# Retention block with two MLPs: sums on VectorE, operand tiles at multiples of 1,024 bytes, scratch in the output staging

## The chip, the core and the metric

One core of a Trainium2 chip runs the whole program: one launch, all inputs in HBM, the result in HBM. The metric is device time in microseconds, as a median of several executions. One further execution is recorded by the hardware profiler; every row below is of that one.

## The reference

```python
def _attn_ref(q, k, v):                       # 4 x 8 heads x 576 x 64
    scores = scale * np.matmul(q, k.transpose(0, 1, 3, 2))
    gamma = 1.0 - 2.0 ** (-5.0 - np.arange(H))
    Dmat = np.where(rel >= 0, gamma[:, None, None] ** rel[None], 0.0)
    return np.matmul(scores * Dmat[None], v)

def _moe_ref(x, w_in, w_out):                 # 2304 x 512, 512 x 2048, 2048 x 512
    h = np.maximum(x @ w_in, 0.0)
    return h * h @ w_out

def _moe2_ref(x, w_gate, w_val, w_out):       # 2304 x 512, 512 x 1536 (twice), 1536 x 512
    g = x @ w_gate
    silu = g * (1.0 / (1.0 + np.exp(-g)))
    return silu * (x @ w_val) @ w_out

def reference(q, k, v, ...):
    x = _attn_ref(q, k, v).transpose(0, 2, 1, 3).reshape(2304, 512)
    return _moe2_ref(_moe_ref(x, ...), ...)
```

## The kernel before

**Three passes for one product.** Operands of the MLPs are kept as pairs, a high part and the rest. `three` (L176 to L178) multiplies a pair by a pair with three matmuls: high by high, high by low, low by high. The moving operand comes from one SBUF tile and the stationary one from another.

**The weights** arrive as 64-bit numbers. `round32` turns a raw tile of 1,024 columns into 32-bit floats (two ScalarE steps, L214 and L219; four VectorE steps, L222, L225, L231, L234), and `split` (L252 on ScalarE, L256 on VectorE) makes the pair. For the first MLP the pairs stay in SBUF (`convert1`, 16 tiles `w`). For the second they go to DRAM (`keep`), twelve gate/value tiles (`convert_gv`) and six output tiles (`convert_out`), while the first MLP runs. `convert_gv` also makes four sums of quarter tiles, at L295, on GpSimd (POOL).

**First part.** Eighteen cells of retention (128 rows each) are woven between the blocks of the first MLP. A block is 512 rows, one of the five 256. For each of 16 slices `f`, `mlp1_h` does 12 matmuls from the tile `x` into the single PSUM bank `hps`; `mlp1_act` does the rest (`relu` on ScalarE into a scratch tile, `square`, `hi`, `lo` on VectorE) and writes the pair `h`; `mlp1_y` does 12 matmuls from `h` into four banks `acc`. In both the weights `w` are the stationary operand. Block results go by way of `yd` in DRAM.

**Second part.** Three blocks of 768 rows times twelve slices make 36 steps. A step's gate and value products are done as seven half-size products (`PRODUCTS`, `mlp2_gv`, matmuls 128x384 from the tiles `xc`), whose sums VectorE takes from PSUM in turn into the banks' successors; then come six pieces of the output product (`mlp2_o`, 128x512, L806 to L808), two steps late. Step 1 has no such pieces, and step 0 has the last pieces of the first MLP. `fetch_x` makes the seven operand tiles `xc` of a block from `yd`: four differences at L621 on GpSimd, seven splits. `xc` has NX = 9 places; part `n` takes the place of part `n - NX`, after that one's last product.

**Order.** `Plan` writes the whole instruction order. Each operation has an engine, an assumed time, dependencies and a rank; a list scheduler picks the operation that can start earliest, the lowest rank first among those that are ready. Every engine then runs its list in order. A 512-column matmul is assumed at 0.2264 us.

**Where tiles lie.** Pools stack from both ends of a partition. The left stack begins at byte 1,152: 1,024 of DMA scratch, and four constants of 32 each. Then come `x` (2 tiles of 16,384), `h` (2 of 4,096), the scratch `tp`, and the staging. The right stack begins at byte 229,344 and grows down, first `pad` (32 bytes), then the weight tiles, 8,192 bytes each. So in the first part `x` and `h` start 128 bytes past a multiple of 1,024, and the weight columns that one matmul loads (512 bytes) start 960 or 448 past one. In the second part `xc`, the weight ring and `at` all lie in the right stack, at 960 or 448 past a multiple.

Of the kernel before, what the change touches and what calls it, by code (L numbers as in the profile page):

```python
# [10 lines left out]
F32 = mybir.dt.float32  # L11
# [17 lines left out]
T2, N2 = 6, 3  # L29
# [11 lines left out]
         ("V", 1), ("raw", 1), ("A", 2), ("q", 2), ("V", 2), ("A", 3), ("q", 3), ("V", 3)]  # L41
PRODUCTS = [("A11", "B11"), ("A12", "B21"), ("S2", "T2"), ("S1", "T1"), ("S3", "T3"), ("S4", "B22"), ("A22", "T4")]
PLAIN, SUMS = ["A11", "A12", "A22"], ["S1", "S2", "S3", "S4"]
NX, NRING = 9, 7
INSERTS = {2: (4, 10), 4: (2, 6, 10, 13)}


# [90 lines left out]
def kernel(ctx: ExitStack, tc: tile.TileContext, units, qtab, tab, w1, w2, out):  # L138
# [11 lines left out]
    do = Plan()  # L150

    pad = ctx.enter_context(tc.tile_pool(name="pad", bufs=1, side="right"))
    pad.tile([128, 8], F32, name="pad")
    wp = ctx.enter_context(tc.tile_pool(name="wp", bufs=NW1 - NA, side="right"))
    wstack = ExitStack()
    wa = wstack.enter_context(tc.tile_pool(name="wa", bufs=NA, side="right"))
    xp = ctx.enter_context(tc.tile_pool(name="xp", bufs=2))
    hp = ctx.enter_context(tc.tile_pool(name="hp", bufs=2))
    tp = ctx.enter_context(tc.tile_pool(name="tp", bufs=1))
    io = ctx.enter_context(tc.tile_pool(name="io", bufs=2))  # L160
    sp = ctx.enter_context(tc.tile_pool(name="sp", bufs=1))
    cv = ctx.enter_context(tc.tile_pool(name="cv", bufs=1))
# [85 lines left out]
    def split(get, n, out, place, rank, deps, cols=None):  # L248

        def hi():  # L250
            out["t"] = place()
            nc.scalar.copy(out=out["t"][:, 0], in_=get())  # L252

        def lo():
            t = out["t"]
            nc.vector.tensor_tensor(out=t[:, 1], in0=get(), in1=t[:, 0].bitcast(F32), op=ALU.subtract)  # L256

        h = do("ACT", 0.17 + 0.43 * n / 512, hi, deps, rank)
        return do("DVE", 0.16 + 0.53 * n / 512, lo, [h], rank)
# [24 lines left out]
    def convert_gv(box, f, rank):  # L284


        st, p4 = round32(box, rank)
        a21, a11, a12, a22 = (slice(256 * i, 256 * i + 256) for i in range(4))

        def add(i, a, b, op, new=False):  # L290
            def go():
                if new:
                    st["s"] = cv.tile([128, 4, 256], F32, tag="r", name="s")
                x, y = (st["s"][:, k] if isinstance(k, int) else st["fm"][:, k] for k in (a, b))
                nc.gpsimd.tensor_tensor(out=st["s"][:, i], in0=x, in1=y, op=op)  # L295
            return go

        s = do("POOL", 0.7, add(0, a21, a22, ALU.add, True), [p4], rank)
        s = do("POOL", 0.7, add(1, 0, a11, ALU.subtract), [s], rank)
        s = do("POOL", 0.7, add(2, a11, a21, ALU.subtract), [s], rank)  # L300
        s = do("POOL", 0.7, add(3, a12, 1, ALU.subtract), [s], rank)
        l = keep("P", f, st, 768, lambda: st["fm"][:, 256:], rank, [p4])
        f_users.append(do("NONE", 0.0, lambda: None, [s, l]))
        r_users.append(keep("S", f, st, 1024, lambda: st["s"].rearrange("p a b -> p (a b)"), rank, [s, l]))
# [189 lines left out]
    def mlp1_act(j, f):  # L494
        n = BLOCKS[j][1] * C
        i = at1[j, f]
        k = n / 512
        st = {}
        on_act = j in (0, NB - 1)

        def relu():
            st["r"] = tp.tile([128, n], F32, tag="t", name="r")
            nc.scalar.activation(out=st["r"], in_=banks[0][:, :n], func=ACTF.Relu)  # L503

        def square():
            if on_act:
                nc.scalar.activation(out=st["r"], in_=st["r"], func=ACTF.Square)
            else:
                nc.vector.tensor_tensor(out=st["r"], in0=st["r"], in1=st["r"], op=ALU.mult)  # L509

        def hi():
            Hs[j, f] = hp.tile([128, 2, n], F32R, tag="h", name="h")
            nc.scalar.copy(out=Hs[j, f][:, 0], in_=st["r"])  # L513

        def lo():
            nc.vector.tensor_tensor(out=Hs[j, f][:, 1], in0=st["r"], in1=Hs[j, f][:, 0].bitcast(F32), op=ALU.subtract)  # L516

        a = do("ACT", 0.17 + 0.43 * k, relu, [h_op[j, f], hlo_op.get(order1[i - 1]) if i else None], -3)
        relu_op[j, f] = a
        if on_act:  # L520
            b = do("ACT", 0.19 + 0.43 * k, square, [a], -2)
        else:
            b = do("DVE", 0.16 + 0.53 * k, square, [a], -2)
        c = do("ACT", 0.19 + 0.43 * k, hi, [b, y_op.get(order1[i - 2]) if i > 1 else None], -2)
        hlo_op[j, f] = do("DVE", 0.16 + 0.53 * k, lo, [c], -2)
# [80 lines left out]
    def fetch_x(b, rank):  # L606

        st = {}

        def load():  # L610
            st["t"] = xp.tile([128, KC + 1, T2 * C], F32, tag="x", name="ys")
            nc.sync.dma_start(out=st["t"][:, :KC], in_=y_dram[b])

        def at(name):
            if name == "T2":
                return st["t"][:, KC].rearrange("p (k n) -> p k n", k=2)
            k, h = {"B11": (0, 0), "B12": (0, 1), "B21": (2, 0), "B22": (2, 1), "T1": (0, 0), "T3": (0, 1), "T4": (2, 0)}[name]
            return st["t"][:, k:k + 2, h * HALF:h * HALF + HALF]

        def sub(o, a, c):  # L620
            return lambda: nc.gpsimd.tensor_tensor(out=at(o), in0=at(a), in1=at(c), op=ALU.subtract)  # L621

        free = [h_op[NB - 2 + b, NF1 - 1]] if b < 2 else [("ysdone", b - 2)]
        ready = {}
        ld = do("SP", 0.4, load, [*y_saved[b], *free, late["open"]], rank, kb=1536)

        def part(i, name, deps):
            n = 7 * b + i
            old = M_op[((n - NX) // 7) * NF2 + NF2 - 1, (n - NX) % 7] if n >= NX else late["open2"]
            out = {}  # L630

            def place():
                XC[b, name] = late["xc"].tile([128, 2, 2, HALF], F32R, tag="xc", name="xc")
                return XC[b, name]

            x_op[b, i] = l = split(lambda: at(name), 2 * HALF, out, place, rank, [*deps, old, *x_chain[-1:]])
            x_chain.append(l)
            return l

        b11 = part(0, "B11", [ld])  # L640
        b21 = part(1, "B21", [ld])
        t1 = do("POOL", 1.95, sub("T1", "B12", "B11"), [b11], rank)
        t2 = do("POOL", 1.95, sub("T2", "B22", "T1"), [t1], rank)
        t3 = do("POOL", 1.95, sub("T3", "B22", "B12"), [t1], rank)
        t4 = do("POOL", 1.95, sub("T4", "B21", "T2"), [t2, b21], rank)
        part(2, "T2", [t2])
        part(3, "T1", [t1])
        part(4, "T3", [t3])
        part(5, "B22", [t3])
        do.named["ysdone", b] = part(6, "T4", [t4])  # L650
# [35 lines left out]
    def mlp2_gv(s, pieces):  # L686
# [15 lines left out]

        def copy(name, bank, pool):
            def go():
                st[name] = late[pool].tile([128, HALF], F32, tag="t" if pool == "tp" else name, name=name)
                nc.scalar.copy(out=st[name], in_=late[bank][:, :HALF])
            return go

# [48 lines left out]

        other(0)
        product(0, "MA", [("c21", s - 1), late["open2"]])
        m1 = do("ACT", act, copy("m1", "MA", "tp"), [M_op[s, 0], ("u2", s - 1) if s else hlo_op[order1[-1]]], -3)  # L760
        product(1, "MB", [("c12", s - 1)])
        c11_ = name("c11", do("DVE", dve, c11, [M_op[s, 1], m1, g_op[s - 2] if s > 1 else y_op[order1[s - 2]]], -3))
        sg = do("ACT", act, sig(0, lo_half), [c11_, ("si1", s - 1)], -2)
# [170 lines left out]
    for j in range(NB):  # L934
# [3 lines left out]
        if not more:  # L938
            def swap():
                astack.close()  # L940
                late["tl"] = ctx.enter_context(tc.tile_pool(name="tl", bufs=1, reuse_waits="tile"))
                pgv = ctx.enter_context(tc.tile_pool(name="pgv", bufs=1, space=PSUM, reuse_waits="tile"))
                late["MA"], late["MB"], more = (pgv.tile([128, 512], F32, name=f"gv{i}") for i in range(3))
                late["more"] = [banks[0], more]
                late["tp"] = tp

            def swap2():
                wstack.close()
                for key, bufs in (("xc", NX), ("rg", 1), ("at", 2), ("tm", 1)):
                    late[key] = ctx.enter_context(tc.tile_pool(name=key, bufs=bufs, side="right", reuse_waits="tile"))  # L950

            late["open"] = do("NONE", 0.0, swap, [*(x for xs_ in x_done.values() for x in xs_), *(st_op[c] for c in range(NC))])
            late["open2"] = do("NONE", 0.0, swap2, [late["open"], y_op[NB - 1, NA - 1]])
# [25 lines left out]
    for s in range(steps2):  # L979
        b, f = divmod(s, NF2)  # L980
        mlp2_gv(s, last_y if s == 0 else () if s == 1 else mlp2_o(s - 2))
        if s == 0:
            fetch_x(0, 60)
        if f == 1 and b + 1 < N2:
            fetch_x(b + 1, 4)
    for s in (steps2 - 2, steps2 - 1):
        for piece in mlp2_o(s):
            piece()
# [69 lines left out]
```

## Time and profile before

| what | us |
|---|---|
| median of 3 runs (lowest to highest) | 931.86 (931.78 to 934.02) |
| profiled execution | 934.56 |
| its span, first to last instruction | 932.8 |
| PE busy in it | 909.2 |
| DVE, ACT, POOL busy | 593.8, 362.3, 120.5 |

The profiled execution lies 2.7 us above the median. PE is TensorE's matmuls, PEld its weight loads, DVE is VectorE, ACT ScalarE, POOL GpSimd. Matmuls overlap in the record: one lasts 0.28 to 0.40 us, while the next begins 0.11 to 0.23 us after it. So what a matmul costs in a stream is read from the starts of successive ones in the timeline, not from its duration. A row of the stretches view gives, for each engine, the busy time in that stretch and the count of instructions, and then TensorE's granted clock, where 1.00 is its upper level (2.4 GHz).

### The profile page before, as it was taken

The page shows a single profiled execution, that of the slowest core. Times are in us where ns is not written, and L with a number is a line of the kernel's source. Part 1 is how long each engine was busy: PE and PEld are TensorE (multiplying, and loading weights), DVE is VectorE, ACT ScalarE, POOL GpSimd, SP SyncE. Part 2 cuts the span into 40 slices and gives each one's busy share as a digit, 9 for nine tenths or more (in the row PEclk, how much of TensorE's full clock was granted, in tenths as well). Part 3 has the DMA queues.
Part 4 walks back from the last instruction along what each step waited for, and adds up shares of the span by engine and source line. Part 5 has one row for each costly group of instructions (what it writes and reads, how often), then busy time and mean ns, then how long its engine had stood idle before and what let it go on. Part 6 is the DMA issues. An engine that isn't in the chain of part 4 may idle for free.

```text
span 932.8 us, 12545 instructions
## 1 busy us (share of the span) xinstructions
PE 909.2 (97%) x4953; PEld 793.7 (85%) x4953; DVE 593.8 (64%) x872; ACT 362.3 (39%) x546; POOL 120.5 (13%) x97
## 2 busy tenths in 40 slices
PE   8899999999999999999999999998999999999997
PEld 7688879988878778878887899998999999999996
DVE  5999836457773777736455655569655557655554
ACT  3678743234541445446553222223222223322221
POOL 3210102112431312301133000003000000000000
PEclk9999999999999999999999999999999999999999
DMA  8665605337673567645436754555555455745521
GB/s 350 226 208 185 227 36 185 123 109 265 236 260 102 177 232 296 226 173 220 181 131 250 297 207 188 219 203 203 199 222 209 187 225 207 277 187 224 208 115 68
DMA packets 36634, 187.49 MB, mean 201 GB/s; under 512 B 4192, under 2 KB 5984, under 8 KB 22624
## 3 DMA queue, kind: packets, MB, share of 16 engines
q1 hardware_dynamic: 36576, 186.70, 53.7%
q8 instruction: 39, 0.64, 0.3%
q14 instruction: 19, 0.16, 0.1%
HBM read 148.93 MB, written 37.75 MB: 200 GB/s over the span
## 4 chain that ended last, share of the span: by engine, by line
PE 88%; DVE 6%; DMA 2%; ACT 2%; issue 2%; SPq 0%; ACTq 0%; DVEq 0%
PE gv L178 9%; PE gv L177 9%; PE gv L176 9%; PE acc L177 7%; PE hps L176 7%; PE acc L176 7%; PE acc L178 7%; PE hps L178 6%; PE hps L177 6%; PE acc L807 4%; PE acc L808 4%; PE acc L806 3%; DMA raw<-w 2%; PE xs L427 2%; PE sc L390 2%
## 5 line engine op out<-in xcount | busy, mean ns | idle before, releaser
L176 PE MATMUL gv<-xc,w 128*128 128x384 f32 x504 | 170.2, 338 | 5.8 <-DVE u L731 3.4
L177 PE MATMUL gv<-xc,w 128*128 128x384 f32 x504 | 171.3, 340 | 0.0
L178 PE MATMUL gv<-xc,w 128*128 128x384 f32 x504 | 171.0, 339 | 0.0
L176 PE MATMUL acc<-h,w 128*128 128x512 f32 (+1 forms) x320 | 119.5, 373 | 2.9 <-ACT yt L573 2.2
L177 PE MATMUL acc<-h,w 128*128 128x512 f32 (+1 forms) x320 | 119.5, 373 | 2.6 <-DVE h L516 2.5
L176 PE MATMUL hps<-x,w 128*128 128x512 f32 (+1 forms) x320 | 120.8, 378 | 1.0 <-ACT r L503 1.0
L177 PE MATMUL hps<-x,w 128*128 128x512 f32 (+1 forms) x320 | 119.1, 372 | 0.9 <-DVE x L452 0.9
L178 PE MATMUL hps<-x,w 128*128 128x512 f32 (+1 forms) x320 | 119.0, 372 | 0.0
L178 PE MATMUL acc<-h,w 128*128 128x512 f32 (+1 forms) x320 | 118.9, 372 | 0.0
L176 PEld LDWEIGHTS gv<-xc,w 128*128 128x128 f32 x504 | 95.5, 189 | 15.7 <-DVE u L731 4.6
L177 PEld LDWEIGHTS gv<-xc,w 128*128 128x128 f32 x504 | 95.3, 189 | 8.2
L736 ACT ACTIVATE sg<-g 128x384 f32<-128x384 f32 x72 | 37.8, 525 | 162.9 <-DVE g L728 131.5
L178 PEld LDWEIGHTS gv<-xc,w 128*128 128x128 f32 x504 | 95.4, 189 | 0.0
L503 ACT ACTIVATE r<-hps 128x512 f32<-128x512 f32 (+1 forms) x80 | 44.4, 555 | 127.1 <-PE hps L178 116.9
L516 DVE TENSOR_TENSOR h<-r,h 128x512 fp32r<-128x512 f32 (+1 forms) x80 | 55.6, 695 | 59.5 <-ACT h L513 59.0
L176 PEld LDWEIGHTS acc<-h,w 128*128 128x128 f32 x320 | 60.1, 188 | 15.9 <-ACT yt L573 2.9
L177 PEld LDWEIGHTS acc<-h,w 128*128 128x128 f32 x320 | 60.1, 188 | 15.3 <-DVE h L516 4.1
L176 PEld LDWEIGHTS hps<-x,w 128*128 128x128 f32 x320 | 60.1, 188 | 14.8 <-ACT r L503 1.9
L177 PEld LDWEIGHTS hps<-x,w 128*128 128x128 f32 x320 | 60.2, 188 | 12.1 <-DVE x L452 1.2
L178 PEld LDWEIGHTS hps<-x,w 128*128 128x128 f32 x320 | 60.1, 188 | 11.5
L178 PEld LDWEIGHTS acc<-h,w 128*128 128x128 f32 x320 | 60.1, 188 | 11.4
L509 DVE TENSOR_TENSOR r<-r 128x512 f32<-128x512 f32 (+1 forms) x48 | 33.2, 692 | 48.2 <-ACT r L503 48.2
(106 smaller groups left out, 1486.6 us busy)
## 6 DMA issues: line engine op xcount, KB each, us to landing
w<-wdS SPq DMA_DIRECT2D x36, 1024.0 KB, 5.7
raw<-w SPq DMA_DIRECT2D x34, 1024.0 KB, 4.8
w<-wdP SPq DMA_DIRECT2D x36, 768.0 KB, 5.8
w<-wdO SPq DMA_DIRECT2D x18, 1024.0 KB, 4.8
wdS<-cw SPq DMA_DIRECT2D x12, 1024.0 KB, 4.2
wdP<-cw SPq DMA_DIRECT2D x12, 768.0 KB, 3.4
qk<-units SPq DMA_DIRECT2D x14, 512.0 KB, 4.4
kv<-units SPq DMA_DIRECT2D x14, 512.0 KB, 3.9
```

The lines of the kernel that those rows point to most:

```text
L176: nc.tensor.matmul(ps, lhsT=wh, rhs=xh, start=first, stop=False)
L177: nc.tensor.matmul(ps, lhsT=wh, rhs=xl, start=False, stop=False)
L178: nc.tensor.matmul(ps, lhsT=wl, rhs=xh, start=False, stop=last)
L390: nc.tensor.matmul(s[h][:, p], lhsT=A[c][r, p, 1], rhs=A[c][r, p, 0], start=True, stop=True)
L427: nc.tensor.matmul(bank("xo")[r, p], lhsT=V[c][:, p, 1, r], rhs=P[c][:, h, p], start=c in FIRST and p == 0, stop=p == NP - 1)
L503: nc.scalar.activation(out=st["r"], in_=banks[0][:, :n], func=ACTF.Relu)
L509: nc.vector.tensor_tensor(out=st["r"], in0=st["r"], in1=st["r"], op=ALU.mult)
L516: nc.vector.tensor_tensor(out=Hs[j, f][:, 1], in0=st["r"], in1=Hs[j, f][:, 0].bitcast(F32), op=ALU.subtract)
L736: nc.scalar.activation(out=t, in_=st["g"][:, r], func=ACTF.Sigmoid)
L806: nc.tensor.matmul(ps, lhsT=at[:, 0, sl], rhs=wh, start=f == 0, stop=False)
L807: nc.tensor.matmul(ps, lhsT=at[:, 0, sl], rhs=wl, start=False, stop=False)
L808: nc.tensor.matmul(ps, lhsT=at[:, 1, sl], rhs=wh, start=False, stop=f == NF2 - 1)
```

## The change

- The sums of `convert_gv` (L295) and the differences of `fetch_x` (L621) are issued on VectorE and no longer on GpSimd.
- `pad` grows to 992 bytes and a `pad2` of 896 bytes opens the left stack. `x` then starts at byte 2,048, the weight stack ends at 228,352; all of `x`, `h`, `w`, `xc`, `at` start at multiples of 1,024, and single operands within them at 0 or 512 past one.
- The pool `tp` goes. The first MLP's scratch comes from `io`, the output staging (two tiles), and the second's `m1` from `tl`.
- `NX` is 11: nine places of `xc` as before and two (`xl`) in the left stack, where the retention's tiles were.
- Blocks 1 and 2 of the second MLP are fetched at rank 60 and not 4; their last three parts stay at 4.

```diff
-NX, NRING = 9, 7
+NX, NXL, NRING = 11, 2, 7
...
-    pad.tile([128, 8], F32, name="pad")
+    pad.tile([128, 248], F32, name="pad")
     wp = ctx.enter_context(tc.tile_pool(name="wp", bufs=NW1 - NA, side="right"))
     wstack = ExitStack()
     wa = wstack.enter_context(tc.tile_pool(name="wa", bufs=NA, side="right"))
+    ctx.enter_context(tc.tile_pool(name="pad2", bufs=1)).tile([128, 224], F32, name="pad2")
     xp = ctx.enter_context(tc.tile_pool(name="xp", bufs=2))
     hp = ctx.enter_context(tc.tile_pool(name="hp", bufs=2))
-    tp = ctx.enter_context(tc.tile_pool(name="tp", bufs=1))
...
-                nc.gpsimd.tensor_tensor(out=st["s"][:, i], in0=x, in1=y, op=op)
+                nc.vector.tensor_tensor(out=st["s"][:, i], in0=x, in1=y, op=op)
...
-        s = do("POOL", 0.7, add(0, a21, a22, ALU.add, True), [p4], rank)
+        s = do("DVE", 0.43, add(0, a21, a22, ALU.add, True), [p4], rank)
...
-            st["r"] = tp.tile([128, n], F32, tag="t", name="r")
+            st["r"] = io.tile([128, n], F32, tag="io", name="r")
...
-            return lambda: nc.gpsimd.tensor_tensor(out=at(o), in0=at(a), in1=at(c), op=ALU.subtract)
+            return lambda: nc.vector.tensor_tensor(out=at(o), in0=at(a), in1=at(c), op=ALU.subtract)
...
-                XC[b, name] = late["xc"].tile([128, 2, 2, HALF], F32R, tag="xc", name="xc")
+                XC[b, name] = late["xl" if n % NX < NXL else "xc"].tile([128, 2, 2, HALF], F32R, tag="xc", name="xc")
...
-            x_op[b, i] = l = split(lambda: at(name), 2 * HALF, out, place, rank, [*deps, old, *x_chain[-1:]])
+            x_op[b, i] = l = split(lambda: at(name), 2 * HALF, out, place, min(rank, 4) if b and i >= NX - 7 else rank,
+                                    [*deps, old, *x_chain[-1:]])
...
-        t1 = do("POOL", 1.95, sub("T1", "B12", "B11"), [b11], rank)
+        t1 = do("DVE", 0.96, sub("T1", "B12", "B11"), [b11], rank)
...
-        m1 = do("ACT", act, copy("m1", "MA", "tp"), [M_op[s, 0], ("u2", s - 1) if s else hlo_op[order1[-1]]], -3)
+        m1 = do("ACT", act, copy("m1", "MA", "tl"), [M_op[s, 0], ("u2", s - 1) if s else hlo_op[order1[-1]]], -3)
...
-                late["tl"] = ctx.enter_context(tc.tile_pool(name="tl", bufs=1, reuse_waits="tile"))
+                for key, bufs in (("tl", 1), ("xl", NXL)):
+                    late[key] = ctx.enter_context(tc.tile_pool(name=key, bufs=bufs, reuse_waits="tile"))
...
-                for key, bufs in (("xc", NX), ("rg", 1), ("at", 2), ("tm", 1)):
+                for key, bufs in (("xc", NX - NXL), ("rg", 1), ("at", 2), ("tm", 1)):
...
-            fetch_x(b + 1, 4)
+            fetch_x(b + 1, 60)
```

## Rows read from the trace of the kernel before

**Rows 1.** The page's first part: busy time, share of the span and instructions.

```profile
PE 909.2 (97%) x4953; PEld 793.7 (85%) x4953; DVE 593.8 (64%) x872; ACT 362.3 (39%) x546; POOL 120.5 (13%) x97
```

**Rows 2.** The chain that ended last, by engine.

```profile
PE 88%; DVE 6%; DMA 2%; ACT 2%; issue 2%; SPq 0%; ACTq 0%; DVEq 0%
```

**Rows 3.** Waits of PE alone: who for whom, us in total, times, longest.

```profile
PE gv L176 <- DVE u L731: 3.4, 2, 2.3
PE acc L177 <- DVE h L516: 2.5, 3, 1.4
```

**Rows 4.** Stretches: blocks 0, 2 and 3; steps 0-1, 2-11 and 12-13.

```profile
31.85:130.85 99.00, 97.36 (x488) 78.19 (x486) 83.60 (x103) 74.87 (x93) 5.33 (x4) 1.00 0.48 170
...
193.72:300.16 106.44, 105.05 (x579) 86.04 (x578) 71.64 (x90) 43.95 (x61) 29.03 (x24) 1.00 0.57 203
300.16:406.15 105.99, 104.80 (x554) 84.84 (x552) 72.38 (x91) 48.67 (x64) 27.33 (x25) 1.00 0.59 221
...
497.25:521.21 23.96, 20.51 (x101) 18.59 (x99) 16.69 (x26) 8.47 (x14) 8.71 (x4) 0.93 0.65 240
521.21:636.85 115.64, 115.64 (x601) 107.58 (x601) 71.17 (x125) 30.37 (x54) 0.00 (x0) 1.00 0.55 209
636.85:664.13 27.28, 24.95 (x121) 22.80 (x120) 23.61 (x32) 9.39 (x16) 7.83 (x4) 0.94 0.54 213
```

**Rows 5.** Groups by form: 512-column matmuls of the first MLP, first of six.

```profile
L176 PE MATMUL hps<-x,w 128*128 128x512 f32 x256 | 102.7, 401 | 1.0 <-ACT r L503 1.0
```

**Rows 6.** Timeline of PE in block 2: two matmuls, twelve apart.

```profile
225.78 0.39 PE L176 MATMUL hps<-x,w 128*128 128x512 f32 x1
...
228.58 0.39 PE L176 MATMUL acc<-h,w 128*128 128x512 f32 x1
```

**Rows 7.** Timeline of PE at the end: two output matmuls, twelve apart.

```profile
919.22 0.39 PE L807 MATMUL acc<-w,at 128*128 128x512 f32 x1
...
921.94 0.39 PE L807 MATMUL acc<-w,at 128*128 128x512 f32 x1
```

**Rows 8.** Timeline of PE in block 1: two 256-column matmuls, twelve apart.

```profile
165.51 0.28 PE L176 MATMUL hps<-x,w 128*128 128x256 f32 x1
...
166.87 0.28 PE L176 MATMUL acc<-h,w 128*128 128x256 f32 x1
```

**Rows 9.** Timeline of PE in a step: starts of two products of six.

```profile
598.70 0.33 PE L176 MATMUL gv<-xc,w 128*128 128x384 f32 x1
...
599.76 0.33 PE L176 MATMUL gv<-xc,w 128*128 128x384 f32 x1
...
600.80 0.39 PE L806 MATMUL gv<-w,at 128*128 128x512 f32 x1
```

**Rows 10.** Groups by form: what moves off POOL.

```profile
L621 POOL TENSOR_TENSOR ys<-ys 128x768 f32<-128x768 f32 x12 | 25.6, 2152 | 180.0 <-DVE xc L256 155.6 <-PE acc L178 24.1
...
L295 POOL TENSOR_TENSOR s<-f 128x256 f32<-128x256 f32 x24 | 25.1, 1047 | 126.0 <-DVE f L234 126.0
...
L295 POOL TENSOR_TENSOR s<-s,f 128x256 f32<-128x256 f32 x12 | 14.7, 1227 | 0.9
...
L295 POOL TENSOR_TENSOR s<-f,s 128x256 f32<-128x256 f32 x12 | 10.7, 892 | 0.0
```

**Rows 11.** Groups by form: VectorE instructions of the moved sizes.

```profile
L256 DVE TENSOR_TENSOR at<-g,at 128x768 fp32r<-128x768 f32 x36 | 34.5, 957 | 27.4 <-ACT at L252 27.3
...
L509 DVE TENSOR_TENSOR r<-r 128x256 f32<-128x256 f32 x16 | 6.8, 426 | 18.4 <-ACT r L503 18.4
```

**Rows 12.** Timeline in step 12, POOL, then DVE; the last row an ordinary step.

```profile
643.06 6.07 POOL L621 TENSOR_TENSOR ys<-ys 128x768 f32<-128x768 f32 x3 [131.39 <-DVE xc L256]
...
643.17 2.16 DVE L718 TENSOR_TENSOR g<-u,m 128x384 f32<-128x384 f32 x1 [0.24 <-ACT m L706]
...
670.45 0.56 DVE L718 TENSOR_TENSOR g<-u,m 128x384 f32<-128x384 f32 x1 [1.60 <-ACT m L706]
```

**Rows 13.** Timeline of DVE in step 1, while POOL makes differences.

```profile
509.89 2.19 DVE L740 TENSOR_TENSOR g<-g,sg 128x384 f32<-128x384 f32 x1
```

More of the change, by code (lines that the diff above doesn't have):

```diff
@@ L294, in go @@
                 x, y = (st["s"][:, k] if isinstance(k, int) else st["fm"][:, k] for k in (a, b))
-                nc.gpsimd.tensor_tensor(out=st["s"][:, i], in0=x, in1=y, op=op)
+                nc.vector.tensor_tensor(out=st["s"][:, i], in0=x, in1=y, op=op)
             return go
-        s = do("POOL", 0.7, add(0, a21, a22, ALU.add, True), [p4], rank)
-        s = do("POOL", 0.7, add(1, 0, a11, ALU.subtract), [s], rank)
-        s = do("POOL", 0.7, add(2, a11, a21, ALU.subtract), [s], rank)
-        s = do("POOL", 0.7, add(3, a12, 1, ALU.subtract), [s], rank)
+        s = do("DVE", 0.43, add(0, a21, a22, ALU.add, True), [p4], rank)
+        s = do("DVE", 0.43, add(1, 0, a11, ALU.subtract), [s], rank)
+        s = do("DVE", 0.43, add(2, a11, a21, ALU.subtract), [s], rank)
+        s = do("DVE", 0.43, add(3, a12, 1, ALU.subtract), [s], rank)
         l = keep("P", f, st, 768, lambda: st["fm"][:, 256:], rank, [p4])
@@ L641, in fetch_x @@
         b21 = part(1, "B21", [ld])
-        t1 = do("POOL", 1.95, sub("T1", "B12", "B11"), [b11], rank)
-        t2 = do("POOL", 1.95, sub("T2", "B22", "T1"), [t1], rank)
-        t3 = do("POOL", 1.95, sub("T3", "B22", "B12"), [t1], rank)
-        t4 = do("POOL", 1.95, sub("T4", "B21", "T2"), [t2, b21], rank)
+        t1 = do("DVE", 0.96, sub("T1", "B12", "B11"), [b11], rank)
+        t2 = do("DVE", 0.96, sub("T2", "B22", "T1"), [t1], rank)
+        t3 = do("DVE", 0.96, sub("T3", "B22", "B12"), [t1], rank)
+        t4 = do("DVE", 0.96, sub("T4", "B21", "T2"), [t2, b21], rank)
         part(2, "T2", [t2])
@@ L704, in go @@
             def go():
-                st[name] = late[pool].tile([128, HALF], F32, tag="t" if pool == "tp" else name, name=name)
+                st[name] = late[pool].tile([128, HALF], F32, tag=name, name=name)
                 nc.scalar.copy(out=st[name], in_=late[bank][:, :HALF])
@@ L944, in swap @@
                 late["more"] = [banks[0], more]
-                late["tp"] = tp
             def swap2():
                 wstack.close()
-                for key, bufs in (("xc", NX), ("rg", 1), ("at", 2), ("tm", 1)):
+                for key, bufs in (("xc", NX - NXL), ("rg", 1), ("at", 2), ("tm", 1)):
                     late[key] = ctx.enter_context(tc.tile_pool(name=key, bufs=bufs, side="right", reuse_waits="tile"))
```

## The prediction

> **What bounds the kernel now.** I read the page's busy times first. PE is busy for 97% of the span and everything else for 64% or less [rows 1]; the chain that ended last is PE for 88% [rows 2]. So a change counts only where it lets PE finish sooner: by ending waits of PE, or by making its own stream denser. The waits of PE are small, the two longest entries being 3.4 and 2.5 us, both for VectorE [rows 3]. By stretches, the ten steps 2 to 11 are an unbroken stream, 115.64 us busy of 115.64, thus 11.56 us a step; steps 12 and 13 took 27.28 us instead of 23.13; steps 0 and 1 took 23.96 with PE busy 20.51 [rows 4]. The rest of the time is the stream itself, so I looked at its density.
>
> A matmul's duration says little, since neighbours overlap (401 ns for 512 columns [rows 5]). The starts say it. In block 2, twelve matmuls of 512 columns take 228.58 - 225.78 = 2.80 us, 233.3 ns each [rows 6]. At the end of the program twelve matmuls of the same form take 921.94 - 919.22 = 2.72 us, 226.7 ns each [rows 7]. The granted clock is 1.00 at both. They differ in where the operands lie. In block 2 the moving operand starts 128 bytes past a multiple of 1,024 and the weights 960 or 448 past one, so that they are 832 or 320 apart, modulo 1,024. At the end both lie at 960 or 448, and are 0 or 512 apart. With 256 columns, at the distances of block 2, twelve take 1.36 us, 113.3 ns each, which is exactly half of 226.7 [rows 8]: that form pays nothing.
>
> **The change part by part.**
>
> *Alignment, first part.* The left stack now starts at 1,152 + 896 = 2,048 and the right one ends at 229,344 - 992 = 228,352 = 223 x 1,024. Moving operands `x` and `h` start at 0, the weights at 0 or 512: a distance of 0 or 512, as at the end of the program. Six groups of 256 matmuls have this form [rows 5], 1,536 in all. If they go from 233.3 to 226.7 ns, that is 1,536 x 6.67 ns = 10.2 us. The bounds are 0 (distance is not the cause) and 10.2; I take 10.2, since the two stretches agree in form, clock and stationary size, and differ in distance. What else differs: in block 2 the operands lie at opposite ends of memory and other engines are busy beside PE. Against it, one charge: a stream needs some matmuls to settle. After a switch of form, six products took 1.06 us and the next six 1.04 [rows 9], 0.02 us for a restart. The ten cells of retention inside 512-row blocks make about 20 restarts: +0.4 us (0.2 to 0.8).
>
> The rule that speaks against this is the Trainium skill's "TensorE: Matmul & The Clock Gate", section "Back-to-back issue gap": the gap is N / 2.4 + 2.5 ns, about 216 ns for 512 columns, whatever the addresses; and "SBUF — State Buffer", section "SBUF: two separate sides", says that TensorE's port never waits for another engine. By both, this part would be worth 0. The trace disagrees so far: it has two spacings for one form, and neither is 216.
>
> *Alignment, second part.* `xc`, ring and `at` already lie 0 or 512 apart, and all move by the same 64 bytes; the two `xl` places, now on the left, are multiples of 1,024 too. I take 0. The bound on either side is the restart of 0.02 us [rows 9], once for each of some 200 switches: 4 us more or less.
>
> *Block 0.* Here VectorE is busy 83.6 of 99.0 us with weights that PE needs in this block [rows 4]. PE's part of the gain is 384 x 6.67 ns = 2.6 us; neither of PE's longest waits is for a weight tile [rows 3], so most of it should fit. I take back 0.5 (0 to 2.6).
>
> *Sums of the weights on VectorE.* 48 instructions leave POOL, 25.1 + 14.7 + 10.7 = 50.5 us there [rows 10]. On VectorE each costs what the nearest form costs, 128x256 at 426 ns [rows 11]: 48 x 0.426 = 20.4 us, in blocks 1 to 4, 1.7 us for each of twelve tiles, and each tile's chain is some 2.5 us shorter. No DMA moves. VectorE is busy 71.64 of 106.44 us in block 2 and 72.38 of 105.99 in block 3 [rows 4], so there are over 30 us free in each, against at most 20 x 0.43 = 8.6 us added. What hides them is that freedom; behind a sum on VectorE's list stand `square` and `lo`, for which PE waits before `acc`, and PE has the 12 matmuls of the next slice, 2.72 us, in hand. If the cover is gone, a tile costs its 1.7 us. PE's waits for `h` are 2.5 us [rows 3], part of which the port shared with POOL may cause, so the bounds are -2.5 and +5 (a quarter of 20.4 exposed); I take 0. POOL's own queue keeps only the retention's products, which no longer stand behind sums.
>
> *Differences of the fetch on VectorE.* Twelve instructions of 2,152 ns [rows 10] become twelve at 957 ns, the same form in a split [rows 11]: 3.8 us of VectorE for each block. In exchange VectorE is no longer held while POOL reads. In step 12 POOL works from 643.06 for 6.07 us; beside it one VectorE sum takes 2.16 us, where the same sum takes 0.56 in an ordinary step [rows 12]. PE's loss there is 27.28 - 23.13 = 4.15 us, some 1.6 of it because the granted clock fell to 0.94 on average [rows 4]: it went to its lower level (1.2 GHz) right after PE had stood still. Eleven places let four parts of block 2 be made early and leave three of block 1 for the last moment rather than five, at low rank. VectorE still gets up to seven splits and four differences about step 12, 10.5 us at 957 ns, where an ordinary step leaves it 11.56 - 7.12 = 4.4 us [rows 4]; they can spread, since block 2 is due at step 24. I take -3.0 (-4.15 to +1).
>
> In steps 0 and 1 the port costs VectorE 1.63 us at one multiplication (2.19 us [rows 13] instead of the 0.56 of that size [rows 12]) and less at others; I bound it by 2.8. But step 1 has no output pieces: there PE's work is only 42 matmuls, 7.3 us at 1.04 us for six [rows 9], as much as VectorE's 7.12, and early parts of block 1 (two splits and four differences more, 5.7 us) may land there. I take -0.5 (-2.8 to +2.9).
>
> *Scratch in the staging, `m1` in `tl`.* Two tiles instead of one; the plan still makes `relu` wait for the last `lo`. 0. In block 4 the evictions share them; the `lo` before has long been done then.
>
> *Sum:* -10.2 + 0.4 + 0 + 0.5 + 0 - 3.0 - 0.5 = -12.8 us. Against the profiled execution, 934.56 - 12.8 = 921.8. That execution lies 2.7 us over the median, so the median comes to 931.86 - 12.8 = 919.1 us.
>
> **The rivals.** *A: distance is not the cause* (opposite ends of memory are, or the traffic beside it). This is also the result of the skill's rule. For it: no run here changes addresses alone. Against it: the pattern in block 2 and block 0 is the same however busy VectorE is, and 256 columns at the same distance pay nothing. What stays is -3.0 - 0.5 = -3.5: 928.4 us. This is also the case in which the change does not do what it says.
>
> *B: VectorE takes part of it back.* PE now runs as dense as the plan assumes (0.2264 us), while some VectorE steps last longer than assumed. Each of the twelve conversions then holds back a `lo` by one sum: 12 x 0.43 = 5.1 us, 924.2 us. For it: PE's waits for `h` exist already [rows 3]. Against it: 30 us free in each block.
>
> *C: slower.* VectorE's list becomes the longer one in blocks 1 to 4: the four sums of a tile stand together ahead of `lo` and PE's 2.72 us in hand are used up elsewhere. Full price 12 x 1.7 = 20.4 us: 919.1 + 20.4 = 939.5 us. It decides the sign when over 12.8 of these 20.4 us are exposed, with A when over 3.5. Against it: VectorE's 68% in blocks 2 and 3.
>
> **How the numbers follow.** The forecast has 0.56, A 0.18, B 0.16, C 0.10. A measurement of this kernel can tell 0.3% from no change, 2.8 us: faster is below 929.1, slower above 934.7. The forecast and B are faster. A's centre is just inside, and the bounds of the steps spread it by 4 us, so 0.11 of it counts as faster and 0.07 as same. C counts as slower. Faster 0.83, same 0.07, slower 0.10. The forecast's own bounds add to 912 at the best (-10.2 + 0.2 - 2.5 - 2.8 - 4.15) and, with several costs together, 926. The range reaches to A: 913 to 929.
>
> **What would show it.** Alignment: in the timeline of blocks 0, 2, 3 and 4, twelve matmuls of 512 columns take 2.72 us; blocks 2 and 3 shrink by 2.5 us each. If they still take 2.80, A holds. Second part: steps 2 to 11 stay at 11.56 us. Sums: VectorE's 128x256 sums at about 0.43 us, and PE's waits for `h` not above some 3 us; if they are 8 or more, B, and above 15, C. Fetch: no VectorE instruction of 128x384 above 0.7 us in steps 1 and 12, steps 12 and 13 near 24 us. The prediction is wrong if the first-part spacing stays, or if PE's new waits exceed 8 us.

## The result and the profile after

The changed kernel takes 917.81 us (median of four runs, 916.38 to 917.94) against 931.82 us for the kernel before (four runs, 930.94 to 934.02): a ratio of 0.9843, with a 95% interval of 0.9823 to 0.9862. That is 14.0 us faster; 919.1 us were forecast. Its profiled execution took 917.87 us, with a span of 916.1.

The page's busy times and the chain by engine, after (compare [rows 1, 2]):

```profile
PE 898.2 (98%) x4953; PEld 792.0 (86%) x4953; DVE 598.7 (65%) x932; ACT 361.0 (39%) x546; POOL 45.1 (5%) x37
...
PE 92%; DVE 3%; DMA 2%; ACT 1%; issue 1%; SPq 0%; ACTq 0%
```

POOL lost 75 us of work and VectorE gained 5, not the 32 that were moved: VectorE's own instructions became shorter. The chain is still PE's, more than before. The stretches of the kernel after, blocks 0 to 4, then steps 0-1, 2-11 and 12-13 (columns as in [rows 4]):

```profile
30.09:126.95 96.86, 95.13 (x488) 78.08 (x486) 83.51 (x103) 74.94 (x93) 5.46 (x4) 1.00 0.50 174
126.95:190.67 63.72, 62.52 (x561) 60.00 (x560) 32.78 (x62) 19.62 (x42) 7.42 (x6) 1.00 0.41 141
190.67:293.37 102.70, 102.70 (x578) 86.08 (x577) 71.72 (x106) 44.02 (x61) 12.17 (x8) 1.00 0.57 210
293.37:398.09 104.72, 102.65 (x553) 84.72 (x552) 73.22 (x110) 47.46 (x64) 6.27 (x5) 1.00 0.58 216
398.09:486.77 88.68, 87.55 (x386) 71.91 (x384) 46.02 (x61) 49.74 (x71) 0.00 (x0) 1.00 0.53 197
486.77:508.37 21.60, 19.12 (x100) 17.21 (x99) 17.39 (x30) 9.09 (x15) 0.00 (x0) 1.00 0.71 268
508.37:624.04 115.67, 115.67 (x601) 107.61 (x602) 72.98 (x127) 30.99 (x55) 0.00 (x0) 1.00 0.55 210
624.04:647.46 23.42, 23.27 (x122) 21.31 (x120) 21.30 (x35) 9.55 (x16) 0.00 (x0) 1.00 0.69 261
```

Beside [rows 4] the reader sees block 2 without any idle time of PE, block 0 shorter by 2.1 us, and steps 12-13 shorter by 3.9 with the clock at 1.00 throughout. The ten steps between did not move. The stream itself, in the timeline of PE in block 2 after, two matmuls twelve apart:

```profile
215.37 0.39 PE L176 MATMUL hps<-x,w 128*128 128x512 f32 x1
...
218.09 0.39 PE L176 MATMUL acc<-h,w 128*128 128x512 f32 x1
```

2.72 us for twelve, 226.7 ns each, where [rows 6] had 2.80. In block 1, where the matmuls have 256 columns, again twelve apart:

```profile
161.25 0.28 PE L176 MATMUL hps<-x,w 128*128 128x256 f32 x1
...
162.69 0.28 PE L176 MATMUL acc<-h,w 128*128 128x256 f32 x1
```

1.44 us for twelve, 120.0 ns each. [rows 8] had 1.36: here the alignment made the stream *slower*, and the prediction had not seen it. The moved sums, as groups by form on VectorE, and then the waits of PE for `h` (compare [rows 10, 11, 3]):

```profile
L621 DVE TENSOR_TENSOR ys<-ys 128x768 f32<-128x768 f32 x12 | 11.4, 954 | 0.2
...
L295 DVE TENSOR_TENSOR s<-f 128x256 f32<-128x256 f32 x24 | 10.1, 420 | 0.2
```

```profile
PE acc L177 <- DVE h L516: 0.5, 2, 0.3
```

They cost what the rows of that size had said (957 and 426 ns), and PE's waits for `h` fell from 2.5 to 0.5 us. In steps 0-1 and 12-13 no VectorE instruction of 128x384 lasted longer than 0.56 us.

### The profile page after: what moved, and what is told of

It reads as the page before. It is cut to its first block, busy times and chain, and to the rows that moved or that the text cites. A ratio compares the mean times of both kernels' runs of the same rounds, so it can differ in the third digit from the quotient of the medians.

```text
span 916.1 us, 12502 instructions
## 1 busy us (share of the span) xinstructions
PE 898.2 (98%) x4953; PEld 792.0 (86%) x4953; DVE 598.7 (65%) x932; ACT 361.0 (39%) x546; POOL 45.1 (5%) x37
## 4 chain that ended last, share of the span: by engine, by line
PE 92%; DVE 3%; DMA 2%; ACT 1%; issue 1%; SPq 0%; ACTq 0%
PE gv L178 9%; PE gv L177 9%; PE gv L176 9%; PE hps L176 7%; PE acc L177 7%; PE acc L176 7%; PE acc L178 7%; PE hps L177 7%; PE hps L178 7%; PE acc L808 4%; PE acc L809 4%; PE acc L807 4%; PE sc L390 2%; PE xs L427 2%; DMA raw<-w 2%; PE xs L417 1%
## 5 line engine op out<-in xcount | busy, mean ns | idle before, releaser
L176 PE MATMUL gv<-xc,w 128*128 128x384 f32 x504 | 169.0, 335 | 2.6 <-DVE u L732 1.4
L177 PE MATMUL gv<-xc,w 128*128 128x384 f32 x504 | 170.5, 338 | 0.0
L176 PE MATMUL hps<-x,w 128*128 128x512 f32 (+1 forms) x320 | 120.0, 375 | 1.7 <-ACT r L503 1.7
L176 PE MATMUL acc<-h,w 128*128 128x512 f32 (+1 forms) x320 | 118.2, 370 | 3.0 <-ACT yt L573 2.3
L177 PE MATMUL hps<-x,w 128*128 128x512 f32 (+1 forms) x320 | 118.1, 369 | 0.9 <-DVE x L452 0.9
L177 PE MATMUL acc<-h,w 128*128 128x512 f32 (+1 forms) x320 | 118.1, 369 | 0.5 <-DVE h L516 0.5
L178 PE MATMUL hps<-x,w 128*128 128x512 f32 (+1 forms) x320 | 117.8, 368 | 0.0
L178 PE MATMUL acc<-h,w 128*128 128x512 f32 (+1 forms) x320 | 117.8, 368 | 0.0
L176 PEld LDWEIGHTS gv<-xc,w 128*128 128x128 f32 x504 | 94.6, 188 | 12.4 <-DVE u L732 2.6
L177 PEld LDWEIGHTS gv<-xc,w 128*128 128x128 f32 x504 | 94.4, 187 | 8.1
L516 DVE TENSOR_TENSOR h<-r,h 128x512 fp32r<-128x512 f32 (+1 forms) x80 | 52.0, 650 | 51.5 <-ACT h L513 50.5
L176 PEld LDWEIGHTS acc<-h,w 128*128 128x128 f32 x320 | 60.3, 188 | 14.5 <-ACT yt L573 3.0
L176 PEld LDWEIGHTS hps<-x,w 128*128 128x128 f32 x320 | 60.2, 188 | 14.3 <-ACT r L503 2.6
L177 PEld LDWEIGHTS acc<-h,w 128*128 128x128 f32 x320 | 60.3, 188 | 10.9 <-DVE h L516 1.2
L177 PEld LDWEIGHTS hps<-x,w 128*128 128x128 f32 x320 | 60.3, 188 | 10.8 <-DVE x L452 1.2
L707 ACT COPY m<-gv 128x384 f32<-128x384 f32 x72 | 34.4, 477 | 77.0 <-PE gv L178 77.0
```

The costliest lines, as they stand in the source:

```text
L176: nc.tensor.matmul(ps, lhsT=wh, rhs=xh, start=first, stop=False)
L177: nc.tensor.matmul(ps, lhsT=wh, rhs=xl, start=False, stop=False)
L178: nc.tensor.matmul(ps, lhsT=wl, rhs=xh, start=False, stop=last)
```

## The experiments

Two theories are to be told apart first: that alignment made the gain (denser matmuls), and that moving the sums made it (fewer waits). Then, for each, what exactly acts: the distance between two operands or the multiple of 1,024; VectorE's freedom from GpSimd or the two more places.

### Each half alone

Alignment alone. The edit to the kernel before:

```diff
-    pad.tile([128, 8], F32, name="pad")
+    pad.tile([128, 248], F32, name="pad")
...
+    ctx.enter_context(tc.tile_pool(name="pad2", bufs=1)).tile([128, 224], F32, name="pad2")
...
-            st["r"] = tp.tile([128, n], F32, tag="t", name="r")
+            st["r"] = io.tile([128, n], F32, tag="io", name="r")
...
```

> The kernel before with the two pads alone (and, to make room, the scratch in the staging and m1 in tl): sums stay on GpSimd, nine places, rank 4. Alignment theory: 512-column matmuls of the first MLP step at 226.7 ns, blocks 0, 2, 3 and 4 shorter by some 2 us each, block 1 longer by 384 x 6.7 ns = 2.6 us as in the changed kernel (120 ns instead of 113.3); steps 0-1 and 12-13 still near 24 and 27 us: 931.8 - 10.2 + 2.6 = 924 us. Rival, the sums did it all: 931 us.

Measured: 926.06 us, ratio 0.9932 (0.9911 to 0.9954). Blocks 1 and 2, then steps 0-1 and 12-13 of this kernel:

```profile
128.00:192.66 64.66, 62.73 (x561) 60.01 (x560) 32.34 (x58) 19.44 (x42) 11.23 (x10) 1.00 0.39 139
192.66:297.52 104.86, 103.61 (x579) 85.84 (x578) 71.37 (x90) 44.24 (x61) 30.25 (x24) 1.00 0.56 206
490.44:513.00 22.56, 19.12 (x101) 17.17 (x99) 16.68 (x26) 8.47 (x14) 8.80 (x4) 1.00 0.69 260
628.66:655.96 27.30, 24.93 (x121) 22.82 (x120) 23.62 (x32) 9.32 (x16) 7.83 (x4) 0.94 0.54 213
```

Steps 12-13 are where they were in [rows 4], 27.3 us, at the same clock of 0.94; block 1 became longer by 1.8 us. The time is 2 us above the expected one: the four blocks with 512 columns gave 7.9 us (table below), not 10.2. The waits of PE for `h`, 2.5 us in [rows 3], are still 1.9:

```profile
PE acc L177 <- DVE h L516: 1.9, 3, 1.0
```

The other half: the changed kernel without its pads.

```diff
-    pad.tile([128, 248], F32, name="pad")
+    pad.tile([128, 8], F32, name="pad")
...
-    ctx.enter_context(tc.tile_pool(name="pad2", bufs=1)).tile([128, 224], F32, name="pad2")
```

> The changed kernel with both pads as before (32 bytes, none on the left): all the rest of the change stays. Alignment theory: 512 columns at 233.3 ns again and 256 columns at 113.3, so 917.8 + 10.2 - 2.6 = 925.4 us, with steps 0-1 and 12-13 as short as in the changed kernel. Two of the eleven places then lie 320 from the ring, at an unknown spacing. Rival, the sums did it all: 918 us.

Measured: 924.33 us, ratio 0.9915 (0.9890 to 0.9940). Every 512-column stretch is back at 233.3 ns, the 256-column block at 113.3. That block, block 1:

```profile
130.07:192.08 62.01, 60.80 (x562) 57.94 (x560) 32.74 (x62) 19.58 (x42) 7.24 (x6) 1.00 0.43 145
```

So the pads are worth 924.33 - 917.81 = 6.5 us in the changed kernel, and 6.3 alone (0.68% of 931.8).

And the sums with nothing else, in the kernel before:

```diff
-                nc.gpsimd.tensor_tensor(out=st["s"][:, i], in0=x, in1=y, op=op)
+                nc.vector.tensor_tensor(out=st["s"][:, i], in0=x, in1=y, op=op)
...
-            return lambda: nc.gpsimd.tensor_tensor(out=at(o), in0=at(a), in1=at(c), op=ALU.subtract)
+            return lambda: nc.vector.tensor_tensor(out=at(o), in0=at(a), in1=at(c), op=ALU.subtract)
...
-        t1 = do("POOL", 1.95, sub("T1", "B12", "B11"), [b11], rank)
+        t1 = do("DVE", 0.96, sub("T1", "B12", "B11"), [b11], rank)
...
```

> The kernel before with both sets of sums on VectorE and nothing else: its addresses, nine places, rank 4, its scratch. If the sums alone make the gain of steps 0-1 and 12-13, about 925 us as without pads; if the two more places and rank 60 were needed, VectorE is crowded at steps 12-13, these stay near 27 us and the time is 928 to 932 us; rival C of the prediction (VectorE's list too long): over 932 us.

Measured: 923.51 us, ratio 0.9903 (0.9889 to 0.9917), 9.0 us. Block 2, steps 0-1 and steps 12-13 of this kernel, then its waits of PE for `h`:

```profile
191.34:296.08 104.74, 104.74 (x579) 86.13 (x577) 71.43 (x106) 44.03 (x61) 10.59 (x8) 1.00 0.55 206
...
492.99:514.56 21.57, 19.02 (x100) 17.13 (x98) 17.28 (x30) 8.36 (x14) 0.00 (x0) 1.00 0.69 263
630.22:653.62 23.40, 23.25 (x121) 21.21 (x119) 21.22 (x35) 9.45 (x16) 0.00 (x0) 1.00 0.70 260
```

```profile
PE acc L177 <- DVE h L516: 0.3, 1, 0.3
```

Steps 12-13 lose nothing more than in the changed kernel, with nine places and rank 4. The halves add up: 0.9932 x 0.9903 = 0.9836, against 0.9843 for both. By stretches of the profiled executions, in us:

| stretch | before | alignment alone | sums alone | both |
|---|---|---|---|---|
| up to block 0 | 31.85 | 31.15 | 30.30 | 30.09 |
| block 0 | 99.00 | 96.85 | 98.97 | 96.86 |
| block 1 (256 columns) | 62.87 | 64.66 | 62.07 | 63.72 |
| block 2 | 106.44 | 104.86 | 104.74 | 102.70 |
| block 3 | 105.99 | 104.20 | 105.81 | 104.72 |
| block 4 | 91.10 | 88.72 | 91.10 | 88.68 |
| steps 0-1 | 23.96 | 22.56 | 21.57 | 21.60 |
| steps 12-13 | 27.28 | 27.30 | 23.40 | 23.42 |

### Distance or multiple

In these two the pads go, every moving tile gets 512 bytes of slack, and each block shifts its operands inside it:

```diff
+OFF1 = [80, 16, 64, 48, 32]
...
-        X[j] = xp.tile([128, KC, 2, BLOCKS[j][1] * C], F32R, tag="x", name="x")
+        n = 2 * KC * BLOCKS[j][1] * C
+        t = xp.tile([128, n + 128], F32R, tag="x", name="x")
+        X[j] = t[:, OFF1[j]:OFF1[j] + n].rearrange("p (k a c) -> p k a c", k=KC, a=2)
```

`h` and `xc` are treated likewise. The distance is the weights' first byte less the moving operand's.

> The changed kernel without pads, and each block's moving operands shifted inside a larger buffer. Distance from the moving operand to the weights, modulo 512: first MLP blocks 0 to 4 at 0, 256, 64, 128, 192; second MLP blocks 0 to 2 at 64, 128, 192. No operand starts at a multiple of 512; block 0 starts at 448 or 960. Theory D, the distance decides: block 0 at 226.7 ns for 512 columns, the others at something else, 233.3 ns if 0 is the only good one; block 1 (256 columns) at 113.3 or 120. Rival M, multiples of 1,024 as such decide: block 0 at 233.3 ns like the others. For 384 columns nothing is known but 173.3 ns at 0; if the distance works on them, steps of the second MLP differ between blocks from 11.55 us.

Measured: 919.51 us (one execution). The timeline of PE in block 0, at distance 0 and with no operand at a multiple of 512 (L177 is the former L176), two matmuls twelve apart; then the stretches of block 0, of block 2 (distance 64), and of the second MLP's steps 2 to 11 (distance 64):

```profile
85.21 0.39 PE L177 MATMUL hps<-x,w 128*128 128x512 f32 x1
...
87.93 0.39 PE L177 MATMUL acc<-h,w 128*128 128x512 f32 x1
```

```profile
30.61:127.44 96.83, 95.08 (x488) 78.13 (x487) 82.62 (x103) 74.83 (x93) 6.06 (x4) 1.00 0.49 174
191.21:296.01 104.80, 104.80 (x579) 86.19 (x578) 71.83 (x106) 43.89 (x61) 11.08 (x8) 1.00 0.56 206
...
512.57:627.58 115.01, 115.01 (x600) 107.22 (x601) 72.94 (x127) 30.99 (x55) 0.00 (x0) 1.00 0.55 211
```

2.72 us again, and block 0 is as short as with aligned tiles. So the multiple of 1,024 is not what counts; the distance is. The operands still lie at opposite ends of memory, beside the same traffic, which ends rival A. Block 2 at distance 64 is as long as without pads (104.74 with the sums alone). And the second MLP, which the prediction had at 0, does answer: 11.50 us a step instead of 11.57.

> As the run before, with first MLP blocks 0 to 4 at distances 256, 128, 384, 448, 320 and second MLP blocks at 256, 320, 384. Theory D: block 4 at 233.3 ns, as every block of the kernel before; the others tell how wide the good region around 0 is: 448 is 64 below 0, and if only the overlap of the two reads counts it is as good as 0. Rival M: all at 233.3 ns. Steps of the second MLP: 11.55 us if the distance does nothing to 384 columns.

Measured: 920.79 us (one execution). The settled spacing (the median over all groups of twelve successive matmuls in a block) in each block of both runs, and the settled step of the second MLP, sorted by distance. The 256 columns at 0 and at 320 are from the kernels with and without pads:

| distance | 512 columns, ns | 256 columns, ns | 384 columns: step, us |
|---|---|---|---|
| 0 and 256 | 226.7 and 226.7 | 120.0 at both | 11.55 at both |
| 64 and 320 | 233.3 and 233.3 | 113.3 at 320 | 11.49 and 11.49 |
| 128 and 384 | 232.6 and 232.6 | 118.8 at 128 | 11.52 and 11.52 |
| 192 and 448 | 228.9 and 228.9 | (next runs) | 11.41 at 192 |

Entries 256 bytes apart agree: only the distance modulo 256 counts, for tiles at multiples of 64. At 128 and 384 the groups of 512 columns scatter, from 231.7 to 233.3 ns; at the others most agree within 0.1 ns. And no distance is best for every column count: 0 is best for 512 and worst for 256.

### Each form at its best distance

The changed kernel with its pads; only the 256-column block and `xc` move:

```diff
+OFFX, OFFXC, OFFAT = 48, 16, (0, 0, 0)
...
+        o = OFFX if BLOCKS[j][1] == 2 else 0
+        t = xp.tile([128, n + o], F32R, tag="x", name="x")
+        X[j] = t[:, o:o + n].rearrange("p (k a c) -> p k a c", k=KC, a=2)
...
+                t = late["xl" if n % NX < NXL else "xc"].tile([128, 4 * HALF + 64], F32R, tag="xc", name="xc")
+                XC[b, name] = t[:, OFFXC:OFFXC + 4 * HALF].rearrange("p (a k c) -> p a k c", a=2, k=2)
```

> The changed kernel with its pads, but each form at its best distance so far: 512 columns of the first MLP stay at 0 (226.7 ns), the 256-column block's operands start 192 bytes later, 64 below the weights modulo 256 (113.3 ns as in the kernel before, not 120), and all places of xc start 64 bytes later (distance 192, where the steps of the second MLP took 11.41 us instead of 11.55). Distance theory with a period of 256: block 1 shorter by 384 x 6.7 ns = 2.6 us, 35 steps by 0.14 us = 4.9 us: 917.8 - 7.5 = 910.3 us. If the gain of the steps hung on the output pieces or on the ring and not on xc, 915 us.

Measured: 910.50 us, ratio 0.9765 (0.9751 to 0.9779), the fastest kernel of this study. Block 1 and steps 2-11:

```profile
126.83:188.66 61.83, 60.62 (x562) 57.85 (x560) 32.88 (x62) 19.56 (x42) 7.93 (x6) 1.00 0.42 146
505.71:619.95 114.24, 114.24 (x601) 106.79 (x602) 72.95 (x127) 31.00 (x55) 0.00 (x0) 1.00 0.55 212
```

63.72 became 61.83, and 115.67 became 114.24. Each of a step's seven products now takes 1.04 us; the four behind output pieces took 1.06 before, as [rows 9] show for one. That is 0.09 of the 0.14 us a step; the rest is in the six output pieces, which together took 4.18 us in the changed kernel's timeline and take 4.13 in this one's.

The same with the stationary operand of the output product shifted:

```diff
+OFFX, OFFXC, OFFAT = 48, 16, (16, 32, 48)
...
-            As[s] = late["at"].tile([128, 2, 2 * HALF], F32R, tag="at", name="at")
+            t = late["at"].tile([128, 4 * HALF + 64], F32R, tag="at", name="at")
+            As[s] = t[:, OFFAT[b]:OFFAT[b] + 4 * HALF].rearrange("p (a c) -> p a c", a=2)
```

> As the run before, and in addition the stationary operand of the output product, at, is shifted by 64, 128 and 192 bytes in blocks 0, 1, 2 of the second MLP (0 in the run before). Distance theory: the step length changes from block to block; if 0 is the best distance for 512 columns here as well, all three blocks have longer steps than 11.41 us, by up to 18 x 6.7 ns = 0.12 us at 64. If the three matmuls of a piece are too few for the distance to matter, 11.41 us throughout.

Measured: 913.33 us (one execution); steps of 11.48, 11.49 and 11.47 us in the three blocks against 11.41. So 0 is the best of the four for the output product too, even in pieces of three matmuls.

And the 256-column block at 192 instead of 64 (`OFFX` 16 for 48):

> The best kernel so far with block 1 (256 columns) at distance 192 modulo 256 instead of 64. So far 256 columns take 120 ns at 0, 119 at 128 and 113.3 at 64. If 512 and 256 columns order the distances oppositely (512: 226.7 at 0, 228.9 at 192, 232.7 at 128, 233.3 at 64), 256 columns take about 118 to 120 ns at 192 and block 1 is 2 us longer, 912.5 us; if only 0 and 128 are bad for them, 113.3 ns and 910.5 us.

Measured: 912.07 us (one execution). Block 1:

```profile
127.17:190.27 63.10, 61.81 (x562) 58.84 (x560) 33.29 (x62) 19.61 (x42) 7.56 (x6) 1.00 0.40 143
```

The table's empty place has no single value: of 324 groups of twelve, 145 step at 117.8 ns, the median, and 94 at 113.3. By the medians the two forms order the distances oppositely: 512 has 0, 192, 128, 64 from best to worst, and 256 has 64, 192, 128, 0.

### What shortened steps 12 and 13

The differences of the fetch back on GpSimd, the rest as changed:

```diff
-            return lambda: nc.vector.tensor_tensor(out=at(o), in0=at(a), in1=at(c), op=ALU.subtract)
+            return lambda: nc.gpsimd.tensor_tensor(out=at(o), in0=at(a), in1=at(c), op=ALU.subtract)
...
-        t1 = do("DVE", 0.96, sub("T1", "B12", "B11"), [b11], rank)
+        t1 = do("POOL", 1.95, sub("T1", "B12", "B11"), [b11], rank)
...
```

> The changed kernel with the differences of the fetch back on GpSimd; the sums of the weights stay on VectorE, addresses and eleven places too. If the port that VectorE shares with GpSimd made the loss of steps 12-13, they lose 3 to 4 us again here and VectorE instructions of 128x384 last up to 2 us: 920 to 922 us. If it was the places, steps 12-13 stay at 23.4 us and the time at 918 us.

Measured: 925.83 us (one execution). Steps 12-13, the differences on POOL in step 12, and VectorE beside them:

```profile
627.09:655.48 28.39, 24.97 (x122) 22.72 (x121) 24.09 (x32) 9.32 (x16) 9.17 (x4) 0.94 0.54 205
```

```profile
629.21 9.25 POOL L621 TENSOR_TENSOR ys<-ys 128x768 f32<-128x768 f32 x4 [127.68 <-ACT at L252]
...
632.95 1.73 DVE L741 TENSOR_TENSOR g<-g,sg 128x384 f32<-128x384 f32 x1
...
634.60 2.21 DVE L719 TENSOR_TENSOR g<-u,m 128x384 f32<-128x384 f32 x1
...
636.73 2.55 DVE L256 TENSOR_TENSOR xc<-ys,xc 128x768 fp32r<-128x768 f32 x1
```

5.0 us lost in these two steps and 2.8 in steps 0-1 (24.43 us): 7.8 of the 8.0 us by which this kernel is slower than the changed one, and more than was expected. A sum that takes 0.56 us when GpSimd is quiet [rows 12] takes 2.21 beside it, and the clock falls again, to 0.94 over steps 12-13 and 0.93 over steps 0-1. The Trainium skill, "SBUF — State Buffer", section "SBUF: two separate sides", says that a VectorE instruction with two SBUF inputs and a GpSimd instruction that reads SBUF exclude one another for a whole instruction. The rows agree: the lengthened ones are such instructions, and each of them ends 0.4 or 0.8 us after the GpSimd difference that was running when it began.

The places and the rank, undone alone:

```diff
-NX, NXL, NRING = 11, 2, 7
+NX, NXL, NRING = 9, 0, 7
...
-            fetch_x(b + 1, 60)
+            fetch_x(b + 1, 4)
```

> The changed kernel with nine places of xc, all in the right stack, and fetches at rank 4, as before; pads, sums on VectorE and scratch as changed. If the eleven places and rank 60 carry part of the gain of steps 12-13 (as the prediction's -3.0 assumed), steps 12-13 take over 24 us and the time is 919 to 921 us. If the sums alone do it, 23.4 us and 917.8 us, the same as the changed kernel.

Measured: 917.60 us (917.12 to 918.10), the same as the changed kernel; so are steps 12-13:

```profile
623.25:646.67 23.42, 23.27 (x121) 21.31 (x119) 21.39 (x35) 9.45 (x16) 0.00 (x0) 1.00 0.71 262
```

The two more places and the rank do nothing that can be measured.

## Why the prediction was right, and where its steps were not

The time fell inside the range, 1.3 us from the forecast, but that closeness is in part luck. The terms were read from the profiled execution of the kernel before, and against it they missed by 3.9 us: 921.8 us forecast, 917.87 measured. Errors in both directions cancelled in part, and that execution's 2.7 us above the median covered most of the rest.

**Alignment, first part: right in mechanism, the spacing exact, the term too large.** 512 columns went from 233.3 to 226.7 ns as the end of the program had shown. But blocks 0, 2, 3 and 4 gained 7.2 us by it (changed kernel against its version without pads: 98.98, 104.74, 105.35 and 91.09 us there), not 10.2 less 0.9 of charges. Block 3 is the gap: 0.6 us instead of 2.6. PE stood still there for 0.8 us without pads and for 2.1 with them. The timeline after shows what is late next there:

```profile
325.40 1.05 ACT L252 CAST cw<-f 128x1024 fp32r<-128x1024 f32 x1 [4.91 <-DMA wdS<-cw]
...
326.36 0.59 ACT L503 ACTIVATE r<-hps 128x512 f32<-128x512 f32 x1
...
327.00 0.50 PE L176 MATMUL hps<-x,w 128*128 128x512 f32 x1 [1.04 <-ACT r L503]
```

ScalarE waits for a store of converted weights, because the pair's single place must be free, and `relu` stands behind that cast in its list. PE waits 1.04 us for `relu`. That a faster PE sees more of the store is an argument; no run changes the store alone. In alignment alone the block took 104.20 us, and in the kernel with nine places, whose edit does not touch this part, 104.01 with that wait at 0.2 us. So some 0.7 us of the gap comes and goes between versions, and its cause stays open.

The charge of 0.4 us for restarts rests on a misread row. The 0.02 us of [rows 9] was taken for a stream that settles after a switch of form; at another distance the product right behind an output piece takes 1.04 us too (the run at 910.50 us). What it showed was the distance, and no run measures a restart in the first part by itself.

**256 columns: wrong.** "That form pays nothing" was read at one distance, 64 modulo 256 (832 or 320), and the sum silently kept it at the new one. There it pays 6.7 ns: block 1 went from 62.01 us without pads to 63.72 with them, +1.7. The row needed, 256 columns at distance 0, was not in the trace of before; the term should have had a bound, and had none.

**Alignment, second part: right.** The distance there did not change, and steps 2-11 took 115.67 us against 115.64. That the absolute position is nothing was bounded with 4 us either way and is now shown. But the distance of `xc`, which the prediction took as already good, was the worst of the four for 384 columns: 192 takes 0.14 us a step less.

**Sums of the weights: size off.** I took 0 with a bound of -2.5; sums alone shorten blocks 1 to 4 by 2.7 us (table). PE's wait for `h`, 2.5 us before and 1.9 with alignment alone, fell to 0.3 with the sums alone and 0.5 in the changed kernel: most of it had been GpSimd's doing. Rivals B and C fall.

**The fetch: sizes off.** Steps 12-13 gave 3.9 us (-3.0 taken, within the bounds), steps 0-1 gave 2.4 (-0.5 taken; the early parts of block 1 did not crowd step 1). The reason given was half wrong: the places have no part in it. And part of the gain is TensorE's clock. In the profiled execution of before it fell in both places [rows 4]; with alignment alone, sums still on GpSimd, it fell in steps 12-13 but not in steps 0-1, which then took 22.56 us and not 23.96. The kernel before took 928.9 us in an execution with a granted clock of 0.999 over the span and 934.8 in one with 0.992; the changed kernel's four had 0.998 or 0.999. So some 3 of the 14.0 us, an estimate from the 928.9 and the median of 931.8, go with these falls of the clock, which come in some executions of the kernel before and not in others.

**The start: not foreseen.** Up to block 0 the changed kernel took 1.8 us less. The kernels of this study took from 29.97 to 31.15 us there, the profiled execution of before 31.85, and that execution lay 2.7 us over its median. How much of the 1.8 is the change's stays open.

By terms: alignment in the four blocks -7.2 (forecast -9.3 with its charges), 256 columns +1.7 (0), weights' sums -2.7 (0), fetch -6.2 (-3.5), and the start -1.8 (0, open): -16.2, where the spans differ by 16.7 and the medians by 14.0.

## What to carry to other kernels

Where PE is dense, read the distance between successive starts of matmuls in the timeline, by form, and compare it with the best stretch of the same form anywhere in the program; here 6.5 us from the pads and 7.3 more from the best distances, 1.5% of the time in all, lay in nothing but where the operands' tiles begin. Choose the distance between the stationary and the moving operand for each column count by measurement, since the best one for 512 columns is the worst for 256. And keep two-input work off GpSimd while VectorE is on the path: here a VectorE sum of 0.56 us lasted up to 2.2 us beside a GpSimd difference of about the same 2.2.

## What the runs showed of the hardware

The step from one matmul to the next, in a settled stream at a granted clock of 1.00, depends on the distance of its operands modulo 256 bytes: 226.7 to 233.3 ns for 512 columns, 113.3 to 120.0 ns for 256. It does not depend on the multiple of 1,024, nor on which ends of memory they lie at. The distance is not always the whole of it: at 192 the 256-column stream has two spacings, 117.8 and 113.3 ns. In the second MLP a better distance for the 384-column products removed the 0.02 us that each one lost after an output piece. Distances that are not multiples of 64 were not tried, and why the column count reverses the order is open; the runs show when the step is longer, not why.

The Trainium skill's "TensorE: Matmul & The Clock Gate", section "Back-to-back issue gap", gives about 216 ns for 512 columns as the gap of an isolated matmul, by a formula without a term for addresses, and about 131 ns as measured in a stream of weight loads and matmuls; the prediction took the first for the stream. No settled stretch here has either, and the addresses moved the step by 6.7 ns; the measurement decides.
